# A woven forward pass: order of probability expansions, key blocks and row transposes, and the border to the next stage

## The chip, the core and the metric

The kernel runs on one core of one Trainium2 chip, in one launch. The core has five engines that work side by side: TensorE (PE in the profile, with its weight loads as PEld), VectorE (DVE), ScalarE (ACT), GpSimd (POOL) and SyncE (SP), which here only issues DMAs. PSUM, where TensorE writes its results, has eight banks, all in use in the stage that the change touches. The metric is the time on the device in microseconds (us), lower is better. A run gives one time; three runs of the kernel before are given below.

## The reference

The kernel computes the output of a gated mix of two attention branches, and the gradients of all its inputs but one for a given gradient of the output. There is one sequence of 2048 tokens of width 576.

```python
def _A_ref(x, wq, wk, wv, wo):          # 32 query heads of width 18, one shared key and value head
    q = (x @ wq).reshape(B, S, H, Dh).transpose(0, 2, 1, 3)
    k = x @ wk
    v = x @ wv
    p = softmax(einsum('bhqd,bkd->bhqk', q, k) * Dh ** (-0.5))
    o = einsum('bhqk,bkd->bhqd', p, v)
    return o.transpose(0, 2, 1, 3).reshape(B, S, H * Dh) @ wo

def _B_ref(x, mem0, Wq, Wk, Wv, Wo, seg_len):   # 32 heads of width 128, segments of 32 tokens
    mem = mem0                                   # 8 memory rows
    for s in range(n_seg):                       # 64 segments, each after the one before
        h = concatenate([mem, x[:, s * 32:(s + 1) * 32]], axis=1)
        q, k, v = (einsum('btd,dhe->bhte', h, W) for W in (Wq, Wk, Wv))
        p = softmax(where(mask, einsum('bhqe,bhke->bhqk', q, k) * scale, -1e9))
        o = einsum('bhqk,bhke->bhqe', p, v)
        o = einsum('bhte,hed->btd', o, Wo)
        mem = o[:, :8]                           # the memory of the next segment
        outs.append(o[:, 8:])
    return concatenate(outs, axis=1)

g = sigmoid((x * gate_w).sum(-1, keepdims=True))
out = g * _A_ref(...) + (1 - g) * _B_ref(...)
grads = vjp(out, grad_out)
```

Branch A is plain attention over all tokens. Branch B is a recurrence: the first eight output rows of a segment are the memory rows of the next one.

## The kernel before

The kernel goes through stages one after the other: preparation and the first projections; the *forward weave*; the *bulk* stage (`b_bulk`), which does branch B's token rows for all segments at once, forward and backward; a backward weave; and the weight gradients. The change touches the forward weave, its end and the start of the bulk stage.

**The weave.** `weave` (L282) runs two generators in turns. The *chain*, `b_chain_fwd` (L343), is branch B's recurrence over the memory rows: 64 segments in series, 16 portions each. The *sweep*, `a_pass1` (L1769), is branch A's forward attention, with row sums and the parts of dq that need the whole row: 64 blocks of 512 query columns, each over 16 tiles of 128 keys, so 1024 steps. Two sweep steps run first, then one portion of the chain and one sweep step alternate. With n the number of the sweep's step and j (0 to 15) the number of the portion in its segment, the portion just ahead of step n has j = n - 2 modulo 16. The order on each engine is the order in which the program issues (the stage is scheduled by hand): each engine works its instructions off in that order, and an instruction that waits holds up those behind it.

**A sweep step n** issues to PE: the two score matmuls of the *next* tile (`a_S`, one buffer of two banks), the two of the gradient (`a_dP`, three buffers), and, at its end, the accumulations of tile n-1 into `a_acc`. ACT takes the exponential of the next tile's scores (`a_E`, L1786, three buffers), DVE two products (`a_W`, L1819, two buffers). After each 16 tiles (n divisible by 16) ACT copies `a_acc` to `a_acs` (L1827), and a generator `a_post` (L1848) works on this block in four pieces, called from the sweep's steps: `half(0)` transposes two quarters of `a_acs` on PE into the PSUM tile `c_x` and copies them to `a_tk` on ACT; the second piece loads the block's queries with two transposing DMAs (L1859); `half(1)` transposes the other two quarters into `c_pj` and copies them on DVE (`evac` with `use="sv"[hf]`, L77 and L79 in the profile); the fourth piece does the arithmetic, on GpSimd but for one reciprocal. The transposes are at L1865. Before the change `half(0)` is called at the start of the steps with n = 3 modulo 16 and `half(1)` at the start of those with n = 14 modulo 16, ahead of everything else in the step; the other pieces are called at the end of steps 10 and 15 modulo 16.

**A segment of the chain**, by portions j, with the names of its tiles: 0, row sums of the segment before (`row_sums`, through `c_pj`, to the state `hm`, L320 and L323); 1 to 3, projection of the keys, `proj("k", 0, ...)` into `c_pj` and `proj("k", 1, ...)` into `c_x`, five blocks of four matmuls each; 4 to 6 the queries; 7 to 11 the values, with the scores in `c_x`, exponential `c_E`, denominators, `c_rd` (DVE) and probabilities `c_pn` (GpSimd) among them; in portion 10 the probabilities are spread to block-diagonal tiles by `expand` on GpSimd (L261): `PBm` for the memory keys, `PBx` for the token keys; 12, the output `po` in `c_x`, first eight matmuls with `PBx`, then eight with `PBm`; 13 to 15, `heads(0, 5)`, `heads(5, 11)`, `heads(11, 16)`: the output projection into `ph`, a tile in `c_pj`, four matmuls for each of its 16 indices. `c_pj` and `c_x` have one buffer (one bank) each, and the transposes of `a_post` are given the same two, since the pool that `a_pass1` gets as `xps` is the chain's.

**The border.** After the last sweep step the last block's `a_post` runs to its end at once, with its arithmetic on DVE (`eng`). In that case the query tile takes a buffer of `a_W`, and `a_tk` is the one buffer that the block before still uses. `b_bulk` (L669) then zeroes four tiles for block-diagonal memory rows (`x_vmB` and `x_kmB`, L675) on DVE, issues its first loads on SP (`load`, L709 for the token rows q, k, dO and v, in chunks of 16 heads, 512 KB each, L697 and L700 for the memory rows) and runs a loop over t, one group of four heads in each turn, software-pipelined over seven turns. In a turn, `trans` transposes the q, k, dO and v of a group on PE (`x_tr`, two buffers) and copies them to SBUF, dO and v on ACT, q and k on DVE; groups t for q and k, t - 2 for dO and v. `st_Om` at t - 3 is the first to read `x_vmB`, `st_Qm` at t - 5 the first to read `x_kmB`.

Of the kernel before, what the change touches and what calls it, by code (L numbers as in the profile page):

```python
# [12 lines left out]
BF16 = mybir.dt.bfloat16  # L13
F32 = mybir.dt.float32
U16 = mybir.dt.uint16
U32 = mybir.dt.uint32
P = 128

D = 576
# [27 lines left out]
class Kern:  # L47
# [295 lines left out]
    def b_chain_fwd(self, keep, sp, psum):  # L343
        nc = self.nc
        NSEG = self.NSEG
        hm = self.hm
        hx = keep.tile([P, 3, 64], F32, name="c_hx")
        PBm = keep.tile([P, 8, 64], BF16, name="c_PBm")
        nc.vector.memset(hx[:], 0.0)
# [63 lines left out]
        for s in range(NSEG):  # L413
# [26 lines left out]
            def proj(w, j, kts):  # L440
                if (w, j) not in pj:
                    pj[w, j] = psum.tile([P, 512], F32, name="c_pj" if w == "v" or j == 0 else "c_x", bufs=1)
                self.proj_part(pj[w, j], h_, self.W[w], j, kts)
                if kts[-1] == NKT - 1 and (w, j) != ("k", 1):
                    self.evac(flat(t2[w], j), pj[w, j][:], use="s")
# [17 lines left out]
            nc.gpsimd.tensor_copy(hist[:, :, s, :], h_[:, 0:NKT, 0:8])  # L463
            if not last:
                put_ride(s + 1)
            proj("k", 0, (0, 1))
            yield
            proj("k", 0, (2, 3, 4))
            proj("k", 1, (0,))
            if wt is not None:  # L470
                stash_end(*wt)
                wt = None
# [1 line left out]
                nc.gpsimd.dma_start(self.pq_dram[s // 4].rearrange("c i q s h x k -> (c i q) (s h x k)")  # L474
                                    .rearrange("p (n z) -> p n z", z=256), z4[:].unsqueeze(1).to_broadcast([P, 8, 256]))
            yield
            proj("k", 1, (1, 2, 3, 4))
            yield
            self.evac(flat(t2["k"], 1), pj["k", 1][:], use="s")
            proj("q", 0, (0, 1, 2, 3))  # L480
# [11 lines left out]
            src = self.mem_T(t2["q"], psum, "c_x", 1)  # L492
# [29 lines left out]
            pn = sp.tile([P, 2, 64], BF16, name="c_pn", bufs=1)  # L522
            nc.gpsimd.tensor_tensor(out=pn[:], in0=Et[:], in1=rd[:].unsqueeze(1).to_broadcast([P, 2, 64]), op=ALU.mult)
            PBx = sp.tile([P, 8, 4, 8], BF16, name="c_PBx", bufs=1)
            self.expand(PBm[:, :, 0:32].rearrange("p u (c q) -> p u c q", q=8), pn[:, 1].rearrange("p (u q) -> p u q", q=8), 8)
            self.expand(PBx[:], pn[:, 0].rearrange("p (u q) -> p u q", q=8), 8)
            nc.gpsimd.dma_start(self.pm_dram[s], pn[:].rearrange("p a b -> p (a b)"))
            proj("v", 1, (0, 1))
            yield
# [139 lines left out]
    def b_bulk(self, wp, vp, kp, sp, psum):  # L669
        nc = self.nc  # L670
        NTT = self.NTT
        mx = self.maskX
        mB = {w: [wp.tile([P, 4, 4, E], BF16, name=f"x_{w}mB{i}") for i in range(2)] for w in ("k", "v")}
        for t in mB["v"] + mB["k"]:
            nc.vector.memset(t[:], 0.0)  # L675
        mT = {}
        C = {}
        NG = NTT * 8
# [34 lines left out]
        BQ = 4  # L713
# [64 lines left out]
        def trans(t, w, nb):  # L778
            tt, g, r, d = view(t)
            pt = psum.tile([P, 4, P], BF16, name="x_tr", bufs=2)  # L780
            for i in range(4):
                self.tr(pt[:, i, :], d[w][:, 4 * (g % 4) + i, :], P)
            o = sp.tile([P, 4, P], BF16, name=f"x_{w}T", bufs=nb)
            self.evac(o[:], pt[:], use="s" if w in ("dO", "v") else "v")
            sc[w + "T", t] = o

        st_QT = lambda t: trans(t, "q", 2)
# [135 lines left out]
                 (5, st_K), (3, st_D), (5, st_KE), (3, st_O), (5, st_Q)]  # L923
        after = {st_O: (("vB", 0), ("v", 0)), st_D: (("mT", 0),), st_KE: (("q", 0), ("dO", 1)), st_Q: (("kB", 0), ("k", 3))}
        later = {}
        load(0, ("q", "k", "mT", "dO"))
        load(1, deep)
        load(0, ("v", "vB", "kB"))
        load(1, ("v", "vB", "kB"))
        load(2, deep + ("mT", "v"))  # L930
        for c in range(3, BQ):
            load(c, deep)
        for t in range(NG + 6):
            if t == NG - 8:
                self.sweep_first()
            sc["D"] = psum.tile([P, 512], F32, name="x_D", bufs=1)
            sc["Sb"] = psum.tile([P, 512], F32, name="x_S", bufs=1)
            for n, st in order:
                if n is None:
                    st(t)  # L940
                    continue
                if 0 <= t - n < NG:
                    st(t - n)
                if st in after and t - n >= 0 and (t - n) % 4 == 3:
                    c = (t - n) // 4
                    for w, wait in after[st]:
                        later.setdefault(t + wait, []).append((c + (BQ if w in deep else 3 if w in ("mT", "v") else 2), (w,)))
                        if wait == 0:
                            load(*later[t].pop())
            if t % 4 == 2 and t // 4 - 2 in range(NTT // 4):  # L950
                self.dl_rows(t // 4 - 2, sp, psum)
            for x in later.pop(t, ()):
                load(*x)
            flush(t >= NG)
# [814 lines left out]
    def a_pass1(self, keep, sp, psum, xps):  # L1769
        nc = self.nc  # L1770
        T, NTT = self.T, self.NTT
        NB = NPR * (T // 512)
        dl_all = self.dl_all
        S, E_, W_ = {}, {}, {}
        QD, load = self.QD, self.load_QD

        def mm_S(n):
            S[n] = psum.tile([P, 2, 512], F32, name="a_S", bufs=1)
            kt = n % 16
            for i in range(2):  # L1780
                r = slice(32 * i, 32 * i + 32)
                self.mm(S[n][:, i, :], lhsT=self.KV[r, kt * P:kt * P + P], rhs=QD[n // 16][r, :], tp=(32 * i, 0))

        def ex(n):
            E_[n] = sp.tile([P, 2, 512], BF16, name="a_E", bufs=3)
            nc.scalar.activation(E_[n][:], S.pop(n)[:], ACT.Exp, scale=SCALEA)  # L1786

        def acc_mm(acc, n, src, st, halves, first, last):
            t = src.pop(n)
            for h in halves:  # L1790
                for g in range(4):
                    self.mm(acc[32 * g:32 * g + 32, 256 * h:256 * h + 256],
                            lhsT=st[:, n % 16, 32 * h:32 * h + 32],
                            rhs=t[:, g % 2, 256 * (g // 2):256 * (g // 2) + 256],
                            start=first and h == 0, stop=last, tp=(0, 32 * g))

        mm_S(0)
        ex(0)
        NP_ = 16 * NB
        acc = None  # L1800
        post = None
        for n in range(NP_ + 1):
            if n < NP_:
                kt = n % 16
                if kt == 11:
                    load(n // 16 + 2)
                if post is not None and kt in (3, 14):
                    next(post)
                if n + 1 < NP_:
                    mm_S(n + 1)  # L1810
                dP = [psum.tile([P, 512], F32, name="a_dP", bufs=3) for _ in range(2)]
                for i in range(2):
                    r = slice(64 + 32 * i, 96 + 32 * i)
                    self.mm(dP[i][:], lhsT=self.KV[r, kt * P:kt * P + P], rhs=QD[n // 16][r, :], tp=(64 + 32 * i, 0))
                if n + 1 < NP_:
                    ex(n + 1)
                W_[n] = sp.tile([P, 2, 512], BF16, name="a_W", bufs=2)
                for i in range(2):
                    nc.vector.tensor_tensor(out=W_[n][:, i, :], in0=dP[i][:], in1=E_[n][:, i, :], op=ALU.mult)  # L1819
            if n > 0:  # L1820
                if n % 16 == 1:
                    acc = psum.tile([P, 512], F32, name="a_acc", bufs=1)
                acc_mm(acc, n - 1, E_, self.VK, (0, 1), n % 16 == 1, False)
                acc_mm(acc, n - 1, W_, self.WK, (1,), False, n % 16 == 0)
                if n % 16 == 0:
                    acs = sp.tile([P, 512], F32, name="a_acs", bufs=1)
                    nc.scalar.copy(acs[:], acc[:])  # L1827
                    bb = n // 16 - 1
                    QD.pop(bb)
                    post = self.a_post(bb, acs, sp, xps, dl_all)  # L1830
            if post is not None and n % 16 in (10, 15):
                if next(post, "end") == "end":
                    post = None
            yield
        for _ in post:
            pass
# [11 lines left out]
    def a_post(self, b, acs, sp, psum, dl_all):  # L1848
# [4 lines left out]
        eng = nc.vector if end else nc.gpsimd  # L1853

        def queries():
            qt = sp.tile([P, 2, 2, P], BF16, name="a_qt", tag="a_W" if end else "a_qt", bufs=2 if end else 1)
            src = self.qs_blk(b, 0)
            for a in range(2):
                nc.sync.dma_start_transpose(qt[:, a], src[a])  # L1859
            return qt  # L1860
# [5 lines left out]
            self.evac(tk[:, :, :, 32 * hf:32 * hf + 32], pt[:].rearrange("p t (g c) -> p t g c", c=32), use="sv"[hf])  # L1866

        if end:
            qt = queries()
        tk = sp.tile([P, 2, 4, 64], F32, name="a_tk", bufs=1)  # L1870
        half(0)
        yield
        if not end:
# [29 lines left out]
        r4 = sp.tile([P, 2, 2, 2, 2], F32, name="a_r4", bufs=2)  # L1903
        for w in range(2):
            eng.tensor_copy(r4[:, :, :, w, :], rl[:, w].rearrange("p t (a i) -> p a t i", i=2))
        q4 = qt[:].rearrange("p a t (b c) -> p (a t b) c", c=32)
        eng.tensor_tensor(out=q4, in0=q4, op=ALU.mult,
                                in1=r4[:].rearrange("p a t w i -> p (a t w i)").unsqueeze(2).to_broadcast([P, 16, 32]))
        dq_.dma_start(self.qs_blk(b, 1).rearrange("a p c -> p a c"), qt[:].rearrange("p a t x -> p a (t x)"))

    def sweep_first(self):
        self.QS = [self.wr.tile([P, 2, 512], BF16, name=f"b_QS{c}", bufs=1) for c in range(2)]
# [350 lines left out]
```

## Time and profile before

| | us |
|---|---|
| median of three runs | 5326.19 |
| the three runs | 5326.19, 5325.88, 5336.03 |
| the profiled execution | 5334.26 |
| its span, first to last instruction | 5332.5 |

Busy time by stage of the profiled execution (us; the stages' limits are read off the timeline):

| stage | from to | PE | DVE | ACT | POOL | DMA share |
|---|---|---|---|---|---|---|
| preparation, first projections | 0 to 420 | 386.69 | 171.27 | 149.49 | 72.32 | 0.60 |
| forward weave | 420 to 2060 | 1577.10 | 1419.32 | 1356.62 | 907.59 | 0.58 |
| border and bulk | 2060 to 2646 | 536.74 | 432.61 | 368.95 | 429.69 | 0.84 |
| backward weave | 2646 to 4307 | 1543.33 | 1405.07 | 1305.99 | 951.24 | 0.84 |
| the rest | 4307 to 5332 | 993.10 | 182.11 | 140.07 | 216.02 | 0.84, then 0.65 |

Busy time is when an engine has an instruction in work; matmuls overlap, so a busy PE need not be one at its peak. The table alone does not price an edit: for that one reads, for a single step, which instruction waits for which.

### The profile page before, as it was taken

To read this page: it belongs to the slowest core of one execution; us is meant where nothing else is said; L and a number is where in the kernel's file an instruction comes from. 1 tells how busy PE (TensorE), PEld (TensorE's weight loads), DVE (VectorE), ACT (ScalarE), POOL (GpSimd) and SP (SyncE) were. 2 spreads that over 40 slices of the span, in tenths; PEclk is the share of its full clock that TensorE was granted. 3 is DMA by queue.
4 is the path that set the end of the run, shared out by engine and by line. 5 is a ranking of instruction groups with operands and counts; after the bars stand their busy time and mean duration, and the time that the engine had idled before them with its cause. 6 is when DMAs were issued, how large, how long until landed. Compare 5 with 4: busy or idle time off the path is not lost. (4 is left out here: it accounts for less than half of the span.)

```text
span 5332.5 us, 214646 instructions
## 1 busy us (share of the span) xinstructions
PE 5036.9 (94%) x91428; PEld 2940.1 (55%) x91428; DVE 3610.4 (68%) x7146; ACT 3321.1 (62%) x4816; POOL 2576.9 (48%) x4890
## 2 busy tenths in 40 slices
PE   7999999999999998999889999999999999999999
PEld 6434555555555555777645555555544467764444
DVE  5337888888888887777678888888888831111112
ACT  4327888888888886666668888878877732111101
POOL 4004555555555555777746666666654321222223
PEclk9999999999999999999999999999999999999999
DMA  6645666656655445888867999899987778976653
GB/s 220 230 178 132 147 142 141 139 144 141 141 146 130 117 113 175 252 256 250 256 180 172 202 196 195 193 190 194 195 173 140 149 163 225 267 230 211 196 174 116
DMA packets 1115762, 961.21 MB, mean 180 GB/s; under 512 B 690738, under 2 KB 942139, under 8 KB 1105202
## 3 DMA queue, kind: packets, MB, share of 16 engines
q1 hardware_dynamic: 1013730, 702.18, 54.6%
q0 software_dynamic: 100928, 245.16, 15.7%
q8 instruction: 715, 11.71, 1.0%
q14 instruction: 245, 2.01, 0.1%
q10 hardware_dynamic: 144, 0.15, 0.0%
HBM read 521.16 MB, written 357.96 MB: 165 GB/s over the span
## 5 line engine op out<-in xcount | busy, mean ns | idle before, releaser
L1982 DVE TENSOR_TENSOR b_dS<-b_dP,b_E 128x512 bf16<-128x512 f32 x2048 | 1314.1, 683 | 235.6 <-issue 97.4
L1819 DVE TENSOR_TENSOR a_W<-a_dP,a_E 128x512 bf16<-128x512 f32 x2048 | 1313.3, 683 | 206.7 <-issue 74.6
L1959 ACT ACTIVATE b_E<-b_S 128x1024 bf16<-128x1024 f32 x1024 | 1047.8, 1023 | 298.5 <-PE b_dP L82 209.1
L1786 ACT ACTIVATE a_E<-a_S 128x1024 bf16<-128x1024 f32 x1024 | 1049.0, 1024 | 239.8 <-PE a_dP L82 192.6
L82 PEld LDWEIGHTS <-b_QS 32*128 32x128 bf16 (+1 forms) x8192 | 269.4, 92 | 529.8 <-issue 461.4
L82 PE MATMUL r_pj<-WT,r_dT 128*32 128x288 bf16 x12288 | 498.0, 287 | 8.4 <-issue 8.3
L82 PE MATMUL b_S<-b_KV,b_QS 32*128 32x512 bf16 x2048 | 406.6, 385 | 97.9 <-ACT b_E L1959 58.9
L82 PE MATMUL w_acc<-w_d,w_h 128*128 128x512 bf16 (+1 forms) x2400 | 473.8, 379 | 0.0
L82 PE MATMUL a_S<-a_QD,l_KV 32*128 32x512 bf16 x2048 | 399.5, 381 | 43.0 <-ACT a_E L1786 21.0
L82 PE MATMUL b_acc<-b_dS,b_QS 128*32 128x512 bf16 x2048 | 425.9, 394 | 0.2
L82 PE MATMUL a_acc<-a_E,l_VK 128*32 128x256 bf16 x8192 | 412.7, 278 | 5.2
L82 PE MATMUL b_acc<-b_E,b_QS 128*32 128x512 bf16 x2048 | 409.5, 395 | 1.5 <-issue 1.5
L82 PE MATMUL b_dP<-b_KV,b_QS 32*128 32x512 bf16 x2048 | 404.5, 390 | 0.0
L82 PE MATMUL a_dP<-a_QD,l_KV 32*128 32x512 bf16 x2048 | 398.4, 385 | 0.1
L82 PEld LDWEIGHTS <-r_dT 128*32 128x32 bf16 x12288 | 336.9, 97 | 100.7 <-issue 14.4
L82 PEld LDWEIGHTS <-w_h 128*128 128x128 bf16 (+1 forms) x2688 | 229.9, 100 | 258.4 <-issue 6.6
L82 PEld LDWEIGHTS <-l_KV 32*128 32x128 bf16 x4096 | 150.2, 91 | 288.5 <-issue 264.6
L82 PE MATMUL a_acc<-a_W,l_WK 128*32 128x256 bf16 x4096 | 291.4, 273 | 0.4 <-DVE a_W L1819 0.3
L79 ACT CAST w_o<-w_acc 128x512 bf16<-128x512 f32 x54 | 31.6, 585 | 384.3 <-PE w_acc L82 358.0
L77 DVE CAST w_o<-w_acc 128x512 bf16<-128x512 f32 x54 | 37.3, 691 | 335.2 <-PE w_acc L82 306.8
L82 PEld LDWEIGHTS <-l_VK 128*32 128x32 bf16 x8192 | 129.3, 94 | 237.1 <-issue 233.3
L1100 POOL TENSOR_TENSOR r_kb<-r_ks,bmask 128x512 bf16<-128x512 bf16 x176 | 188.7, 1072 | 146.6 <-DMA r_ks<-px_dram 59.1
(484 smaller groups left out, 10798.6 us busy)
## 6 DMA issues: line engine op xcount, KB each, us to landing
b_QS<-qs_dram SPq DMA_DIRECT2D x256, 256.0 KB
dOx_dram<-p_tok SPq DMA_DIRECT2D x16, 1024.0 KB
c_vx<-vx_dram SPq DMA_DIRECT2D x64, 256.0 KB
krow_dram<-c_k POOLq DMA_DIRECT2D x64, 256.0 KB
qrow_dram<-c_q POOLq DMA_DIRECT2D x64, 256.0 KB
vrow_dram<-c_v POOLq DMA_DIRECT2D x64, 256.0 KB
x_q<-qx_dram SPq DMA_DIRECT2D x32, 512.0 KB
x_k<-kx_dram SPq DMA_DIRECT2D x32, 512.0 KB
```

The lines of the kernel that those rows point to most:

```text
L77: nc.vector.tensor_copy(out, in_)
L79: nc.scalar.copy(out, in_)
L82: return self.nc.tensor.matmul(out, lhsT, rhs, start=start, stop=stop, tile_position=tp, skip_group_check=True)
L1100: nc.gpsimd.tensor_tensor(out=B[:], in0=a[:].unsqueeze(2).to_broadcast([P, 4, 4, SEG]), in1=self.bmask[:, :, 0].unsqueeze(1).unsqueeze(3). ...
L1786: nc.scalar.activation(E_[n][:], S.pop(n)[:], ACT.Exp, scale=SCALEA)
L1819: nc.vector.tensor_tensor(out=W_[n][:, i, :], in0=dP[i][:], in1=E_[n][:, i, :], op=ALU.mult)
L1959: nc.scalar.activation(E_[n][:], S.pop(n)[:], ACT.Exp, scale=SCALEA)
L1982: nc.vector.tensor_tensor(out=D_[n][:, i, :], in0=dP[i][:], in1=E_[n][:, i, :], op=ALU.mult)
```

## The change

Six edits, all in the order of work; what is computed stays the same.

1. In portion 10 `PBx` is spread ahead of `PBm`.
2. The key projections are split over portions 1 to 3 as three, four and three blocks, before as two, four and four.
3. `half(0)` is called at the end of the steps n = 2 modulo 16 (before at the start of the following one), `half(1)` at the end of the steps n = 14 modulo 16 (before at their start).
4. The last block's query tile is loaded five steps ahead of the sweep's end into a buffer of the chain's `c_wt`, whose weights are all through by then, and its `a_tk` takes a buffer of `a_E`.
5. In the bulk loop the four memsets and the loads that need them move into the turns t = 0 to 3 (`first`), one in each; the token rows v of chunk 0 are loaded ahead of chunk 1, and the loads of chunk 1's v and of the chunks 2 and 3 are issued from turns 0 to 2.
6. For t = 0 all copies of `trans` go to ACT.

```diff
--- before.py
+++ after.py
@@ -344,6 +344,7 @@
         nc = self.nc
         NSEG = self.NSEG
         hm = self.hm
+        self.cfs = sp
         hx = keep.tile([P, 3, 64], F32, name="c_hx")
         PBm = keep.tile([P, 8, 64], BF16, name="c_PBm")
         nc.vector.memset(hx[:], 0.0)
@@ -463,10 +464,10 @@
             nc.gpsimd.tensor_copy(hist[:, :, s, :], h_[:, 0:NKT, 0:8])
             if not last:
                 put_ride(s + 1)
-            proj("k", 0, (0, 1))
-            yield
-            proj("k", 0, (2, 3, 4))
-            proj("k", 1, (0,))
+            proj("k", 0, (0, 1, 2))
+            yield
+            proj("k", 0, (3, 4))
+            proj("k", 1, (0, 1))
             if wt is not None:
                 stash_end(*wt)
                 wt = None
@@ -474,7 +475,7 @@
                 nc.gpsimd.dma_start(self.pq_dram[s // 4].rearrange("c i q s h x k -> (c i q) (s h x k)")
                                     .rearrange("p (n z) -> p n z", z=256), z4[:].unsqueeze(1).to_broadcast([P, 8, 256]))
             yield
-            proj("k", 1, (1, 2, 3, 4))
+            proj("k", 1, (2, 3, 4))
             yield
             self.evac(flat(t2["k"], 1), pj["k", 1][:], use="s")
             proj("q", 0, (0, 1, 2, 3))
@@ -522,8 +523,8 @@
             pn = sp.tile([P, 2, 64], BF16, name="c_pn", bufs=1)
             nc.gpsimd.tensor_tensor(out=pn[:], in0=Et[:], in1=rd[:].unsqueeze(1).to_broadcast([P, 2, 64]), op=ALU.mult)
             PBx = sp.tile([P, 8, 4, 8], BF16, name="c_PBx", bufs=1)
+            self.expand(PBx[:], pn[:, 0].rearrange("p (u q) -> p u q", q=8), 8)
             self.expand(PBm[:, :, 0:32].rearrange("p u (c q) -> p u c q", q=8), pn[:, 1].rearrange("p (u q) -> p u q", q=8), 8)
-            self.expand(PBx[:], pn[:, 0].rearrange("p (u q) -> p u q", q=8), 8)
             nc.gpsimd.dma_start(self.pm_dram[s], pn[:].rearrange("p a b -> p (a b)"))
             proj("v", 1, (0, 1))
             yield
@@ -671,8 +672,6 @@
         NTT = self.NTT
         mx = self.maskX
         mB = {w: [wp.tile([P, 4, 4, E], BF16, name=f"x_{w}mB{i}") for i in range(2)] for w in ("k", "v")}
-        for t in mB["v"] + mB["k"]:
-            nc.vector.memset(t[:], 0.0)
         mT = {}
         C = {}
         NG = NTT * 8
@@ -781,7 +780,7 @@
             for i in range(4):
                 self.tr(pt[:, i, :], d[w][:, 4 * (g % 4) + i, :], P)
             o = sp.tile([P, 4, P], BF16, name=f"x_{w}T", bufs=nb)
-            self.evac(o[:], pt[:], use="s" if w in ("dO", "v") else "v")
+            self.evac(o[:], pt[:], use="s" if w in ("dO", "v") or t == 0 else "v")
             sc[w + "T", t] = o
 
         st_QT = lambda t: trans(t, "q", 2)
@@ -923,13 +922,22 @@
                  (5, st_K), (3, st_D), (5, st_KE), (3, st_O), (5, st_Q)]
         after = {st_O: (("vB", 0), ("v", 0)), st_D: (("mT", 0),), st_KE: (("q", 0), ("dO", 1)), st_Q: (("kB", 0), ("k", 3))}
         later = {}
-        load(0, ("q", "k", "mT", "dO"))
+        load(0, ("q", "k", "mT", "dO", "v"))
         load(1, deep)
-        load(0, ("v", "vB", "kB"))
-        load(1, ("v", "vB", "kB"))
-        load(2, deep + ("mT", "v"))
-        for c in range(3, BQ):
-            load(c, deep)
+
+        def first(t):
+            if t < 4:
+                nc.vector.memset(mB["vk"[t // 2]][t % 2][:], 0.0)
+                load(t % 2, ("vk"[t // 2] + "B",))
+            if t == 0:
+                load(1, ("v",))
+            elif t == 1:
+                load(2, deep)
+            elif t == 2:
+                load(2, ("mT", "v"))
+                for c in range(3, BQ):
+                    load(c, deep)
+
         for t in range(NG + 6):
             if t == NG - 8:
                 self.sweep_first()
@@ -947,6 +955,7 @@
                         later.setdefault(t + wait, []).append((c + (BQ if w in deep else 3 if w in ("mT", "v") else 2), (w,)))
                         if wait == 0:
                             load(*later[t].pop())
+            first(t)
             if t % 4 == 2 and t // 4 - 2 in range(NTT // 4):
                 self.dl_rows(t // 4 - 2, sp, psum)
             for x in later.pop(t, ()):
@@ -1804,8 +1813,11 @@
                 kt = n % 16
                 if kt == 11:
                     load(n // 16 + 2)
-                if post is not None and kt in (3, 14):
-                    next(post)
+                if n == NP_ - 5:
+                    self.qt_last = self.cfs.tile([P, D], BF16, name="c_wt", bufs=2)[:, 0:512].rearrange(
+                        "p (a t x) -> p a t x", a=2, t=2)
+                    for a, src in enumerate(self.qs_blk(NB - 1, 0)):
+                        nc.sync.dma_start_transpose(self.qt_last[:, a], src)
                 if n + 1 < NP_:
                     mm_S(n + 1)
                 dP = [psum.tile([P, 512], F32, name="a_dP", bufs=3) for _ in range(2)]
@@ -1828,7 +1840,9 @@
                     bb = n // 16 - 1
                     QD.pop(bb)
                     post = self.a_post(bb, acs, sp, xps, dl_all)
-            if post is not None and n % 16 in (10, 15):
+            if post is not None and n % 16 in (2, 14):
+                next(post)
+            elif post is not None and n % 16 in (10, 15):
                 if next(post, "end") == "end":
                     post = None
             yield
@@ -1853,7 +1867,7 @@
         eng = nc.vector if end else nc.gpsimd
 
         def queries():
-            qt = sp.tile([P, 2, 2, P], BF16, name="a_qt", tag="a_W" if end else "a_qt", bufs=2 if end else 1)
+            qt = sp.tile([P, 2, 2, P], BF16, name="a_qt", bufs=1)
             src = self.qs_blk(b, 0)
             for a in range(2):
                 nc.sync.dma_start_transpose(qt[:, a], src[a])
@@ -1866,8 +1880,8 @@
             self.evac(tk[:, :, :, 32 * hf:32 * hf + 32], pt[:].rearrange("p t (g c) -> p t g c", c=32), use="sv"[hf])
 
         if end:
-            qt = queries()
-        tk = sp.tile([P, 2, 4, 64], F32, name="a_tk", bufs=1)
+            qt = self.qt_last
+        tk = sp.tile([P, 2, 4, 64], F32, name="a_tk", tag="a_E" if end else "a_tk", bufs=3 if end else 1)
         half(0)
         yield
         if not end:
@@ -1903,10 +1917,11 @@
         r4 = sp.tile([P, 2, 2, 2, 2], F32, name="a_r4", bufs=2)
         for w in range(2):
             eng.tensor_copy(r4[:, :, :, w, :], rl[:, w].rearrange("p t (a i) -> p a t i", i=2))
-        q4 = qt[:].rearrange("p a t (b c) -> p (a t b) c", c=32)
+        qt = qt if end else qt[:]
+        q4 = qt.rearrange("p a t (b c) -> p (a t b) c", c=32)
         eng.tensor_tensor(out=q4, in0=q4, op=ALU.mult,
                                 in1=r4[:].rearrange("p a t w i -> p (a t w i)").unsqueeze(2).to_broadcast([P, 16, 32]))
-        dq_.dma_start(self.qs_blk(b, 1).rearrange("a p c -> p a c"), qt[:].rearrange("p a t x -> p a (t x)"))
+        dq_.dma_start(self.qs_blk(b, 1).rearrange("a p c -> p a c"), qt.rearrange("p a t x -> p a (t x)"))
 
     def sweep_first(self):
         self.QS = [self.wr.tile([P, 2, 512], BF16, name=f"b_QS{c}", bufs=1) for c in range(2)]
```

## What is expected: the prediction

> **What bounds the kernel now.** I read the page's busy table first (TensorE has work for 94% of the span), then the stretches by stage, then the timeline of single steps, since a mean over the span cannot price an edit inside one step. Two stretches of the table by windows, with span, PE, PEld, DVE, ACT and POOL busy, granted clock, DMA share and GB/s, and the border between the forward weave and the bulk stage beneath:
>
> ```profile
> 440.00:800.00 360.00, 346.97 (x7750) 189.66 (x7750) 312.80 (x564) 299.30 (x396) 199.32 (x459) 1.00 0.63 141
> 1600.00:2040.00 440.00, 424.44 (x9440) 231.65 (x9443) 381.53 (x690) 364.96 (x482) 239.28 (x552) 1.00 0.47 116
> 2060.00:2080.00 20.00, 5.59 (x76) 4.43 (x77) 11.05 (x28) 2.21 (x5) 11.29 (x17) 0.50 0.93 297
> ```
>
> In the weave no engine is full: PE 96%, DVE 87%, ACT 83%. At the border PE does 5.6 us of work in 20 us, at half the granted clock, while DMA runs at 0.93.
>
> The weave's steps are all visible as starts of the two a_S matmuls (one pair per step). Over the segment from 1199.75 they lie 1.55, 1.55, 1.55, 1.55, 1.58, 1.55, 1.84, 1.56, 1.55, 1.55, 1.55, 1.60, 1.63, 1.63, 1.63, 1.63 us apart: 25.50 us, and the 63 intervals between the first and the last a_acs copy (448.2 and 2058.2) give 25.56. A segment near 702 and one near 1503 show the same list, but for one step of 1.83 in the latter. The value 1.55 is a floor: a_S starts, 0.48 us later the exponential starts, runs 1.02 us, and the next a_S may enter the one a_S buffer about 0.05 us after that. Only steps whose TensorE work is longer stand above it. A step has about 0.67 us of the sweep's own PE work (from a_S to the chain's first matmul: 1219.39 less 1218.73), 0.22 us for each block of four projection matmuls (1219.39, 1219.82, 1220.04) and about 0.1 us back to a_S; four blocks make 1.63.
>
> The timeline (start, duration, engine, line, operation, count, idle before) from the step where the token values are read. I number steps by the sweep's index modulo 16; a step's interval runs from its a_S to the next, so step 13's begins at 1209.08, step 14's at 1210.92:
>
> ```profile
> 1208.88 0.63 POOL L261 TENSOR_TENSOR c_PBm<-c_pn,bmask 128x256 bf16<-128x256 bf16 x1
> ...
> 1209.08 0.39 PE L82 MATMUL a_S<-a_QD,l_KV 32*128 32x512 bf16 x2
> ...
> 1209.46 0.63 POOL L261 TENSOR_TENSOR c_PBx<-c_pn,bmask 128x256 bf16<-128x256 bf16 x1
> ...
> 1210.15 0.35 PE L82 MATMUL c_x<-c_PBx,c_vx 128*128 128x32 bf16 x8 [0.23 <-POOL c_PBx L261]
> ...
> 1210.35 0.39 PE L82 MATMUL c_x<-c_PBm,c_v 128*128 128x64 bf16 x8
> ...
> 1210.58 0.41 PE L1865 MATMUL c_pj<-identF,a_acs 128*128 128x128 f32 x2
> ...
> 1210.92 0.39 PE L82 MATMUL a_S<-a_QD,l_KV 32*128 32x512 bf16 x2
> ...
> 1211.10 0.42 DVE L77 COPY a_tk<-c_pj 128x256 f32<-128x256 f32 x1 [0.21 <-PE c_pj L1865]
> ...
> 1211.44 1.29 DVE L1819 TENSOR_TENSOR a_W<-a_dP,a_E 128x512 bf16<-128x512 f32 x2
> ...
> 1211.59 0.79 PE L82 MATMUL c_pj<-WoN,c_oT 128*32 128x288 bf16 x20
> ...
> 1212.48 0.39 PE L82 MATMUL a_S<-a_QD,l_KV 32*128 32x512 bf16 x2
> ```
>
> Read four things in it. PE waits 0.23 us for c_PBx, the second of two expansions. The sweep's second pair of row transposes writes c_pj ahead of a_S. Its copy runs on DVE ahead of step 14's two products a_W. And heads, 20 matmuls at 1211.59, write c_pj as well, long after that copy is done.
>
> **Part by part, for a segment.** *Expansions swapped.* PBx would be ready at 1209.51 instead of 1210.09, PBm at 1210.09 instead of 1209.51. The first eight matmuls then start where the sweep's work ends (about 1209.75), the other eight at 1210.15, and end near 1210.38. With the transposes gone from this step, a_S could come at 1210.48, so the floor decides: 1.55 for 1.84, **-0.29 us**. If the second wait reaches a_S, -0.15.
>
> *Second pair of transposes to the end of step 14.* They now stand behind the sweep's accumulations, and right ahead of heads. Heads' tile has c_pj's only buffer, so its first matmul waits for the a_tk copy. That copy is issued behind both products of step 14 on DVE, which runs in the order of issue. Times from the a_S of step 14 at 1209.08 + 1.55 = 1210.63: the products start 0.52 later (1211.44 less 1210.92), at 1211.15, and take 1.29, to 1212.44; the copy follows 0.08 before their end as now, 1212.36 to 1212.78; PE is released 0.06 later (the last a_W ends at 2057.79 and its matmul starts at 2057.85). Heads start at 1212.84. The transposes end near 1211.30 + 0.37 = 1211.67, so PE stands for about 1.15 us, with heads, the next a_S and all after it queued behind. Heads take 20 x 0.03 = 0.6 us (its 20 weight loads take 0.57), 0.1 to a_S: 1213.55. The step is 2.92 for 1.56, **+1.36 us**. Nothing hides it: ACT and DVE then wait for a_S and a_dP, and no later step can be under 1.55. Bounds: +1.05 if the copy starts 0.3 earlier than reckoned, +1.5 if the gaps of the step of 1.83 come on top.
>
> *First pair and keys.* The pair moves from behind the two k blocks to ahead of them, in the same interval (step 2), so the move itself costs nothing there; a_tk's ACT copy stays between the same two exponentials. But this step takes three key blocks for two: 1.60 + 0.22 = 1.82. Step 3 keeps four blocks. Step 4 has three for four: 1.63 to the floor, 1.55. Together **+0.14 us**; bounds +0.02 (a gap of 0.1 before the transposes closes) and +0.21.
>
> Sum: -0.29 + 1.36 + 0.14 = +1.21 us. Heads follow the transposes in segments 1 to 62: 62 x 1.21 = **+75 us**. Bounds 62 x (1.05 - 0.29 + 0.02) = +48 and 62 x (1.5 - 0.15 + 0.21) = +97.
>
> *Border.* What ends each wait of PE there now:
>
> ```profile
> 2061.98 0.42 DVE L77 COPY a_tk<-c_pj 128x256 f32<-128x256 f32 x1 [4.07 <-POOL a_t L1899]
> ...
> 2070.25 0.91 DVE L675 MEMSET x_kmB<- 128x1024 uint32 x1 [0.16 <-issue]
> ...
> 2071.49 0.59 PE L87 MATMUL x_tr<-identB,x_q 128*128 128x128 bf16 x4 [5.13 <-DVE x_qT L77]
> ...
> 2078.47 0.61 PE L87 MATMUL x_tr<-identB,x_v 128*128 128x128 bf16 x4 [3.88 <-DMA x_v<-vx_dram]
> ```
>
> The last block's a_tk in a buffer of the a_E ring starts 2.4 us earlier (its transposes end about 2059.5). The first tile's q and k copies go to ACT, idle then, and one memset instead of four (1.07 us from start to start) stands ahead of the next ones: DVE is free for those at about 2065.6 for 2072.1. But then x_v ends the wait: it is issued at 2064.86, behind three 512 KB loads of the next chunk; ahead of them, at about 300 GB/s, it lands 3 x 1.7 = 5.2 us earlier. The query transposes, on SP until 2059.45, are issued five steps earlier, so all loads may leave SP up to some 6 us sooner if nothing but the queue holds them, which no row shows. Against that, three memsets go into steps 1 to 3 of the bulk loop, and SP's loads of chunks 2 and 3 wait behind the masked-row loads that wait for them. I take **-7 us**, between the 5.2 and the sum of both, and bounds of -12 and +3 (3 x 1.07, if they all show and the loads gain nothing).
>
> The profiled execution took 5334.26 us, its span is 5332.5; the median of the three runs is 5326.19, 8 us below it. Span: 5332.5 + 75 - 7 = 5400.5. On the median: 5326 + 68 = **5394 us**.
>
> **Rivals.** *No wait at heads.* Then step 14 is 0.67 + 0.37 + 0.1 + 0.6 + 0.1 = 1.84, +0.28, a segment -0.29 + 0.28 + 0.14 = +0.13, in all 62 x 0.13 - 7 = +1: **5327 us**, no change; if step 2 gives its 0.14 back too, about 5318. It decides where step 14 costs less than 0.26 us more than now, so the copy would have to be done by about 1211.7, ahead of both products. For it: today's copy starts as soon as its transposes are done. Against: today it is issued ahead of the products, and DVE's rows follow the issue order throughout. 5 in 100.
>
> *The clock drops in each wait.* At the border, after a gap of 4.8 us, four x_tr transposes take 0.61 us at a clock of 0.50 where they take 0.40 at 1.00. If the 2.9 us of PE work in steps 14 and 15 ran at half clock, that is up to 2 us a segment more: 5394 + 124 = **5518 us**. Against: after a gap of 1.58 us at 2100.42 the four transposes still take 0.40. The Trainium skill (TensorE: Matmul & The Clock Gate, The HAM clock gate) puts the drop after an idle window of about 3.4 us, which agrees with both gaps here; its section on psum-queue depth-cycling, though, lets frequent short waits on PSUM buffers make the clock oscillate, which is what this rival would be. 4 in 100.
>
> *The border gives nothing,* since DMA is full there (0.93 share) and x_v still ends the wait: 5326 + 75 = **5401 us**. 6 in 100.
>
> **How the numbers follow.** The forecast has 85 in 100. With the border's bounds its range is 5326 + 48 - 12 = 5362 to 5326 + 97 + 3 = 5426; I take 5360 to 5426, which holds the third rival and leaves out the first two. About 0.2%, 10.7 us, is what a measurement of this kernel can tell from no change: slower 0.95, and of the first rival's share 0.03 within it and 0.02 faster.
>
> **What would show it.** In the changed trace: heads' c_pj matmuls idle about 1.1 us on DVE a_tk, 62 times; a_tk<-c_pj starting behind two a_W; the c_PBx wait of PE (14.2 us in all) gone; a_acs copies 26.8 us apart; the clock 1.00 throughout the weave; no wait of PE for x_v near 3.9 us. If the a_acs copies lie 25.6 us apart, the wait isn't there and the forecast is wrong; if the weave's clock falls below 1.00, the second rival holds.

## The result, and the profile after

| | before | changed |
|---|---|---|
| median | 5330.31 us | 5406.02 us |
| lowest to highest | 5325.88 to 5336.03 | 5403.06 to 5412.49 |
| span of the profiled execution | 5332.5 us | 5404.4 us |

The changed kernel is slower by 1.4%: ratio 1.0141, 95% interval 1.0129 to 1.0154, some 76 us. (The kernel before was run again beside the changed one, which moved its median from 5326.19 to 5330.31.)

Where the 71.9 us between the two spans lie, by marks that both timelines have:

| from | to | before | changed | difference |
|---|---|---|---|---|
| first a_acs copy | last a_acs copy (63 blocks) | 1610.0 | 1690.8 | +80.8 |
| last a_acs copy | first exponential of the bulk stage | 14.7 | 4.3 | -10.4 |
| first exponential | last exponential of the bulk stage | 554.4 | 571.6 | +17.2 |
| last exponential | last accumulation of the backward weave | 1679.2 | 1664.9 | -14.3 |

The first line is the weave, and the second the border. The four differences add up to 73.3; the rest of the program took 1.4 us less. The last two are not the change's work alone: both stages vary from kernel to kernel by such amounts (*The border alone*, below).

The stretches of the changed kernel that answer to those shown of before (span, PE, PEld, DVE, ACT, POOL busy, granted clock, DMA share, GB/s); the border now lies 80 us later:

```profile
440.00:800.00 360.00, 336.33 (x7360) 183.01 (x7362) 297.69 (x539) 282.13 (x375) 191.21 (x441) 1.00 0.58 134
1600.00:2040.00 440.00, 411.87 (x9002) 223.40 (x9005) 362.65 (x656) 343.89 (x457) 235.81 (x544) 1.00 0.49 117
2140.00:2160.00 20.00, 10.71 (x165) 9.10 (x165) 14.21 (x43) 5.59 (x12) 14.71 (x23) 0.59 0.82 262
```

All three engines of the weave lost ground, PE from 347 to 336 us in the first stretch, DVE from 313 to 298, ACT from 299 to 282: no engine became full, and all three stand idle for longer. The clock stays at 1.00. At the border PE does 10.7 us of work in 20 for 5.6.

Steps 13 and 14 of a segment in the changed kernel's timeline, the answer to the rows shown of before. Step 13 begins with the first a_S, step 14 with the second:

```profile
1219.96 0.63 POOL L261 TENSOR_TENSOR c_PBx<-c_pn,bmask 128x256 bf16<-128x256 bf16 x1
...
1220.41 0.39 PE L82 MATMUL a_S<-a_QD,l_KV 32*128 32x512 bf16 x2
...
1220.55 0.63 POOL L261 TENSOR_TENSOR c_PBm<-c_pn,bmask 128x256 bf16<-128x256 bf16 x1
...
1221.18 0.37 PE L82 MATMUL c_x<-c_PBx,c_vx 128*128 128x32 bf16 x8
...
1221.96 0.39 PE L82 MATMUL a_S<-a_QD,l_KV 32*128 32x512 bf16 x2 [0.17 <-ACT a_E L1795]
...
1222.48 1.29 DVE L1831 TENSOR_TENSOR a_W<-a_dP,a_E 128x512 bf16<-128x512 f32 x2 [0.26 <-ACT c_oT L543]
...
1222.73 0.44 PE L1879 MATMUL c_pj<-identF,a_acs 128*128 128x128 f32 x2
...
1223.69 0.41 DVE L77 COPY a_tk<-c_pj 128x256 f32<-128x256 f32 x1
...
1224.16 0.80 PE L82 MATMUL c_pj<-WoN,c_oT 128*32 128x288 bf16 x20 [0.99 <-DVE a_tk L77]
...
1224.89 0.39 PE L82 MATMUL a_S<-a_QD,l_KV 32*128 32x512 bf16 x2
```

The transposes start at 1222.73 and would be ready for their copy half a microsecond later (0.55 us, in the run *The copy ahead of the products* below). The copy starts at 1223.69, 0.08 us ahead of the recorded end of the two products (1222.48 + 1.29). Heads start 0.06 us after its end, having held PE up for 0.99 us, and the next a_S stands behind heads. Step 13 is 1.55 us now, step 14 2.93.

From the waits between 440 and 2110 us (who waits for whom, us in total, times, longest):

```profile
PE c_pj L82 <- DVE a_tk L77: 60.1, 61, 1.0
...
PE c_x L82 <- POOL c_PBm L261: 0.7, 3, 0.2
```

The first is new, 61 waits of about 1 us; with the one behind this window they are 62, 61.1 us in all. The second is what is left of the 14.2 us that PE waited for an expansion.

### The profile page after: what moved, and what is told of

The parts are those of the page before. It is cut to its first block, busy times and chain, and to the rows that moved or that the text cites. A ratio compares the mean times of both kernels' runs of the same rounds, so it can differ in the third digit from the quotient of the medians.

```text
span 5404.4 us, 214473 instructions
## 1 busy us (share of the span) xinstructions
PE 5051.7 (93%) x91250; PEld 2951.4 (55%) x91428; DVE 3608.8 (67%) x7144; ACT 3312.7 (61%) x4818; POOL 2577.4 (48%) x4890
```

## The experiments

All are compared with the kernel before, run on the same chip. "A block" is the distance of the first and the last a_acs copy over 63, in the profiled execution.

**The second pair back.** In the changed kernel, only `half(1)` returns to the start of its step.

```diff
+                if post is not None and kt == 14:
+                    next(post)
                 if n + 1 < NP_:
                     mm_S(n + 1)
...
-            if post is not None and n % 16 in (2, 14):
+            if post is not None and n % 16 == 2:
```

> The changed kernel with its second pair of transposes back at the start of step 14, everything else as changed. Theory (heads wait for the pair's copy, which stands behind two products on DVE): steps 13 and 14 are 1.57 to 1.65 and 1.55 us, the wait of heads for a_tk is gone, a block of the weave takes 25.5 to 25.6 us (26.84 changed, 25.56 before), and the whole is within 10 us of before (5315 to 5332). Rival (the cost lies in the longer step 2 and in the swapped expansions): the kernel stays slower than before by more than 50 us.

Measured: 5333.25 us for 5334.65, ratio 0.9996 (0.9986 to 1.0006). A block takes 25.58 us, step 13 1.64, step 14 1.55, and of PE's waits on c_pj for a copy none is left. The same place (the step's a_S starts at 1209.88):

```profile
1210.06 0.42 DVE L77 COPY a_tk<-c_pj 128x256 f32<-128x256 f32 x1
...
1210.55 0.79 PE L82 MATMUL c_pj<-WoN,c_oT 128*32 128x288 bf16 x20
```

The copy is over at 1210.48, and heads start without a wait. The whole loss is gone with this one edit, and so is the rival. (The time lies 1 us above the 5315 to 5332 that was expected, on a chip on which the kernel before took 5334.65.)

**The second pair alone**, in the kernel before:

```diff
-                if post is not None and kt in (3, 14):
+                if post is not None and kt == 3:
                     next(post)
...
-            if post is not None and n % 16 in (10, 15):
+            if post is not None and n % 16 == 14:
+                next(post)
+            elif post is not None and n % 16 in (10, 15):
```

> The kernel before with nothing but the second pair moved to the end of step 14. Theory: step 13 falls from 1.84 to about 1.60, step 14 goes from 1.56 to 2.9; a block takes 26.6 to 26.75 us, the whole 66 to 74 us more than before (5396 to 5404). Rival (the pair alone is harmless, the cost comes with the other edits): under 20 us more.

Measured: 5401.97 for 5334.65, ratio 1.0138 (1.0125 to 1.0152), 67 us. A block takes 26.66 us, step 13 1.59 (median), step 14 2.92; the wait of heads is there 62 times, 61.3 us. Together with the run before, the loss is placed from both sides: without this edit it is gone, and this edit alone gives 67 of the 76 us.

**The copy ahead of the products.** The changed kernel; on PE the order stays, on DVE the two products of step 14 are issued after the copy.

```diff
-                W_[n] = sp.tile([P, 2, 512], BF16, name="a_W", bufs=2)
-                for i in range(2):
-                    nc.vector.tensor_tensor(out=W_[n][:, i, :], in0=dP[i][:], in1=E_[n][:, i, :], op=ALU.mult)
+                def products():
+                    ...
+                late = post is not None and kt == 14
+                if not late:
+                    products()
...
             if post is not None and n % 16 in (2, 14):
                 next(post)
+                if n % 16 == 14:
+                    products()
```

> The changed kernel, but in step 14 the two products are issued on DVE behind the pair's copy; the order on PE is as changed. Theory (it is the place in DVE's queue): the copy starts 0.5 us after the transposes, step 14 falls from 2.92 to about 2.5 us, with heads' wait at 0.5 to 0.6 for 0.99; 62 x 0.42 = 26 us less than the changed kernel (about 5380). Rival (what costs is handing c_pj over at this place on PE, whatever DVE's order): step 14 stays at 2.9 and the time at 5406.

Measured: 5386.85 for 5334.65, ratio 1.0103 (1.0086 to 1.0119). That is 52 us above the kernel before, for 76: 24 less, where 26 had been expected. Step 14 takes 2.52 us, a block 26.49 for 26.84. The same place in its timeline (the step's a_S starts at 1211.74):

```profile
1212.51 0.44 PE L1886 MATMUL c_pj<-identF,a_acs 128*128 128x128 f32 x2
1213.06 0.42 DVE L77 COPY a_tk<-c_pj 128x256 f32<-128x256 f32 x1 [1.06 <-PE c_pj L1886]
...
1213.40 1.28 DVE L1832 TENSOR_TENSOR a_W<-a_dP,a_E 128x512 bf16<-128x512 f32 x2
1213.54 0.80 PE L82 MATMUL c_pj<-WoN,c_oT 128*32 128x288 bf16 x20 [0.58 <-ACT c_vmT L79]
```

The copy now starts 0.55 us after the transposes, not 0.96, and heads again 0.06 us after its end (1213.48). The profile names an ACT copy of c_x as what released heads; that copy ends 0.03 us later and works on another bank, so it is a case of several ends close together, not a second cause: in the next run heads start 0.22 us before that copy ends. In each of the 62 segments heads start 0.051 to 0.054 us after the end of the a_tk copy, here, there and in the changed kernel. 0.41 of the 1.36 us are thus the place in DVE's queue. What is left, transposes and copy between the accumulations and heads, stays whatever the order on DVE. Heads in a bank of their own were not tried: all eight are in use.

**The copy on ACT.** The changed kernel with `use="ss"[hf]` for `use="sv"[hf]`.

> The changed kernel with the second pair's copy on ACT in place of DVE, at the same place in the order. Theory (the copy waits for whatever is queued ahead on its engine: on ACT the exponential of step 14, which ends 1.50 us after a_S): the copy runs from 1.50 to 1.87, heads start at 1.93, step 14 takes 2.66 us for 2.92; 16 us less than the changed kernel, about 5390. Rival (the wait belongs to the handing over of c_pj): 2.92, no change.

Measured: 5391.94 for 5333.63, ratio 1.0099 (1.0072 to 1.0126). Step 14 takes 2.54 us, 0.12 less than expected: its a_S is at 1210.26, and the copy starts 0.10 us ahead of the exponential's recorded end (1211.75), as the copies on DVE start 0.08 ahead of that of the products:

```profile
1210.73 1.02 ACT L1795 ACTIVATE a_E<-a_S 128x1024 bf16<-128x1024 f32 x1 [0.16 <-PE a_dP L82]
...
1211.65 0.37 ACT L79 COPY a_tk<-c_pj 128x256 f32<-128x256 f32 x1
...
1211.90 0.39 ACT L79 CAST c_vmT<-c_x 128x256 bf16<-128x256 f32 x1
...
1212.07 0.80 PE L82 MATMUL c_pj<-WoN,c_oT 128*32 128x288 bf16 x20 [0.61 <-ACT a_tk L79]
```

So the copy runs from 1.39 to 1.76 after a_S where I had reckoned 1.50 to 1.87. (The cast shown is the copy of c_x of the run before; heads start while it runs.) Heads wait for whichever engine has the copy, by as much as that engine has queued ahead of it.

**The swapped expansions alone**, in the kernel before.

> The kernel before with the swapped expansions alone. Theory: step 13 falls from 1.84 to 1.64 us, no wait of PE for an expansion, 62 x 0.2 = 12 us less (ratio 0.9977). Rival: the other eight matmuls wait as long for the second expansion, step 13 stays above 1.75, no change.

Measured: 5318.63 for 5327.28, ratio 0.9983 (0.9972 to 0.9994). Step 13 takes 1.64 us, a block 25.36 for 25.56: 63 x 0.19 = 12 us by the timeline, 9 by the times.

**The first pair alone**, in the kernel before (`half(0)` to the end of step 2, keys in 2, 4, 4).

> The kernel before with the first pair of transposes alone moved, from behind the key blocks to ahead of them. Theory (a change of tile form on PE in either direction costs about 0.1 us, and this order has one more of them before a_S): step 2 goes from 1.60 to 1.68 us, 5 us more in all. Rival, the prediction's own reading (the move costs nothing): step 2 stays at 1.60.

Measured: 5336.68 for 5327.28, ratio 1.0014 (1.0005 to 1.0023). Step 2 takes 1.68 us, a block 25.65: 6 us in all by the timeline, 9 by the times. PE in step 2, first in the kernel before, then in the changed kernel, which has three key blocks there (x12):

```profile
1217.13 0.39 PE L82 MATMUL a_S<-a_QD,l_KV 32*128 32x512 bf16 x2
...
1217.81 0.61 PE L82 MATMUL c_pj<-Wk,hm 128*32 128x512 bf16 x8
1218.36 0.44 PE L1865 MATMUL c_x<-identF,a_acs 128*128 128x128 f32 x2
1218.73 0.39 PE L82 MATMUL a_S<-a_QD,l_KV 32*128 32x512 bf16 x2
```

```profile
1202.48 0.39 PE L82 MATMUL a_S<-a_QD,l_KV 32*128 32x512 bf16 x2
...
1203.24 0.44 PE L1879 MATMUL c_x<-identF,a_acs 128*128 128x128 f32 x2
1203.61 0.83 PE L82 MATMUL c_pj<-Wk,hm 128*32 128x512 bf16 x12
1204.38 0.39 PE L82 MATMUL a_S<-a_QD,l_KV 32*128 32x512 bf16 x2
```

Read the form behind each MATMUL: 128*32 is a matmul on a strip of 32 columns, 128*128 one on the whole array, 32*128 one on a strip of 32 rows. From the accumulations (128*32 too) to the keys there is no gap, from two key blocks (0.43 us, as from 1219.39 to 1219.82 in the kernel before) to the transposes 0.12, from the transposes (0.37) to a_S none. In the changed order the transposes come 0.76 after a_S where the keys came after 0.68, and from three key blocks (0.65) to a_S there is 0.12 again. So each end of work in strips of 32 columns costs about 0.1 us, and the moved pair makes two such ends out of one; that the other direction costs as much, as the expectation had it, these rows don't show. The Trainium skill (TensorEngine Tiling (Array Packing), Key Properties) says that a change of the tiling mode drains TensorE; the rows agree with that where the strips end and show no gap where the transposes end. Why the two differ was not tried.

**The keys alone**, in the kernel before.

> The kernel before with the keys in 3, 4, 3 alone. Theory: step 2 goes from 1.60 to 1.82, step 4 from 1.63 to 1.55, 0.14 us a block or 9 us in all. Rival (the block just changes its step): no change in the sum of the steps 2 to 4, 4.86 us.

Measured: 5335.75 for 5327.28, ratio 1.0014 (1.0003 to 1.0024). Steps 2 to 4 take 1.82, 1.63, 1.55, a block 25.70: +0.14 us, 9 us in all by the timeline and 8 by the times.

**The border alone**, in the kernel before (edits 4 to 6).

> The kernel before with the three edits of the border alone. Theory: the first exponential of the bulk stage comes 9 to 11 us earlier after the last block's row sums, the fifth about 5 us; the whole gains 5 us (5 to 10). Rival (the bulk stage gives it back, as in the changed kernel's profile, where the lead is gone by the middle of that stage): no change within 3 us, with the bulk stage 5 to 14 us longer than before.

Measured: 5333.50 for 5334.65, ratio 0.9998 (0.9986 to 1.0009). Exponentials of the bulk stage, us after the last a_acs copy:

| | 1st | 3rd | 5th | 9th | 33rd | last |
|---|---|---|---|---|---|---|
| before | 14.7 | 24.5 | 32.2 | 50.7 | 155.9 | 569.1 |
| expansions alone (border as before) | 14.7 | 24.9 | 32.7 | 50.3 | 155.1 | 568.9 |
| second pair alone (border as before) | 14.7 | 23.6 | 31.4 | 49.0 | 155.2 | 578.5 |
| border alone | 3.4 | 16.9 | 27.4 | 44.1 | 151.4 | 579.5 |
| changed kernel | 4.3 | 17.0 | 27.1 | 44.9 | 152.2 | 576.0 |

The lead is 11 us at the first exponential, 5 at the fifth and about 4 at the 33rd. The stage then takes 576.1 us for 554.4 from its first exponential to its last. At the end of the stage kernels with the same border differ by 10 us, and on the mean nothing is left of it: the last exponential comes at 573.8 in the five kernels of all these runs with the border of before, at 573.9 in six with the changed one (without the last run below, whose profiled execution was its slowest). From the last a_acs copy to the end of the program the former take 3262.9 to 3274.4 us, mean 3269.4, the latter 3262.4 to 3276.4, mean 3270.5. That is what the rival says, but the scatter of 10 us could hide a gain of 4 or 5, and the interval of the time (7.5 us less to 4.8 more) holds both.

**The changed border with the swapped expansions**, without the pairs and the keys.

> The kernel before with the swapped expansions and the border's edits, without the moved pairs and the keys in 3, 4, 3. Theory (the two edits add up, step 13 at 1.64 as with the second pair put back): a block takes 25.35 us, the weave 12 us less, the border's net gain 0 to 5: 12 to 17 us less than before (ratio 0.9968 to 0.9978). Rival (the freed 0.2 us is eaten by the wait for the second expansion or elsewhere in the weave): within 5 us of before.

Measured: 5312.77 for 5327.28, ratio 0.9974 (0.9964 to 0.9984). This version beats both kernels, by 14.5 us the one before. From the run with the expansions alone, on the same chip, it differs by the border's edits only: 5312.77 for 5318.63, 6 us less. That is their largest gain on record, but the executions of the latter lie between 5307 and 5331, so it is not certain.

**The first probabilities on DVE**, on top of that, to find what eats the lead. In the changed kernel's border, whose x_v no longer holds PE up:

```profile
2148.90 0.63 PE L87 MATMUL x_tr<-identB,x_v 128*128 128x128 bf16 x4
...
2151.93 0.79 POOL L1924 DMA_DIRECT2D qs_dram<-c_wt  x1
2152.67 0.69 POOL L824 TENSOR_TENSOR x_P<-x_E,x_r 128x256 bf16<-128x256 bf16 x1
2153.41 0.10 PEld L87 LDWEIGHTS <-x_P 128*128 128x128 bf16 x1 [3.27 <-POOL x_P L824]
2153.42 0.29 PE L87 MATMUL x_S<-identB,x_P 128*128 128x128 bf16 x1 [3.01 <-POOL x_P L824]
```

GpSimd still issues the weave's last DMAs, the line shown being the last of a row of them that starts at 2146.44, and x_P stands behind them.

```diff
-            nc.gpsimd.tensor_tensor(out=o[:, t % 4], in0=Et[:], in1=bc(rl[:]), op=ALU.mult)
+            (nc.gpsimd if t else nc.vector).tensor_tensor(out=o[:, t % 4], in0=Et[:], in1=bc(rl[:]), op=ALU.mult)
```

> The swapped expansions and the border's edits, and the probabilities of the bulk stage's first group on DVE in place of GpSimd. Theory (there GpSimd still issues the weave's last DMAs, and x_P behind them holds PE up for 3 us): PE's wait of 3 us for x_P is gone, the fifth exponential of the bulk stage comes 2 to 3 us earlier after the last row sums than without it; 2 to 3 us less, which the time may not tell (ratio 0.997). Rival (another wait takes its place, a load of the masked rows): the fifth exponential comes as before.

Measured: 5321.21 for 5333.63, ratio 0.9975 (0.9961 to 0.9988), no better than without it. The wait for x_P is gone and the third exponential comes at 14.3 us, not 16.9. But the fifth comes at 29.2, not 27.4 (in an execution of 5340 us, the slowest of this kernel):

```profile
2062.66 0.67 POOL L824 TENSOR_TENSOR x_P<-x_E,x_r 128x256 bf16<-128x256 bf16 x1
2069.93 0.61 POOL L886 TENSOR_TENSOR x_Y<-x_P,x_dl 128x256 f32<-128x256 bf16 x1 [6.60 <-DMA memT_dram<-memT_hist]
2070.63 0.72 POOL L888 TENSOR_TENSOR x_dS<-x_X,x_Y 128x256 bf16<-128x256 f32 x1
2071.31 0.67 POOL L749 TENSOR_TENSOR x_PTB<-x_PT,tmask 128x256 bf16<-128x256 bf16 x1
...
2072.03 0.64 PE L82 MATMUL x_po<-x_v,x_PTB 64*64 64x128 bf16 x8 [4.07 <-POOL x_PTB L749]
```

Now x_Y is reached early, and waits 6.6 us for a DMA that the weave's end issued (the profile puts it down to the 640 KB of memT_hist); x_PTB is queued behind it, and PE waits 4.07 us for that. The rival held, with another wait than the one it named. But the later fifth exponential isn't the edit's doing alone: with the second pair back, where x_P still stands on GpSimd, x_Y waits 5.0 us for the same DMA and the fifth comes at 30.1. In all seven kernels with the changed border x_Y starts 19.7 to 21.9 us after the last a_acs copy, whether x_P starts at 10.4 (here) or at 13.6 to 13.7 (the six others). What x_Y shares with memT_hist was not tried.

## Why the prediction was right

**Second pair.** Right, in mechanism and size: step 14 at 2.92 us, as forecast; heads idle 0.99 us for 1.15, 62 times. The wait is shorter because the transposes start 0.77 us after a_S, not 0.67, and their record is longer (0.44 for 0.37); its end, set by DVE, is where it was reckoned (2.20 after a_S for 2.21), and that alone sets the step. Two runs place the loss on this edit, two others 0.4 us of it on the queue ahead of the copy.

**Expansions.** Right in the sum: step 13 came down to the floor of 1.55. But the -0.29 us is not the swap's alone. The pair's leaving by itself brings 1.84 to 1.59, the swap by itself to 1.64; the two gains overlap at the floor, and beside the moved pair the swap is worth 0.04.

**First pair and keys.** Step 4 went to 1.55 as said. The step that failed is "so the move itself costs nothing there": step 2 took 1.90, not 1.82. The gaps around work in 32-column strips had been taken as one constant 0.1 us a step; they depend on what stands next to what, and the move alone costs 0.08. Together +0.22 us a block, not +0.14, and just beyond the bound of +0.21.

**The sum of the weave.** 1.28 us a block instead of 1.21, so 80.8 us instead of 75: the 0.08 of the first pair over 62 blocks is 5 us of it.

**Border.** The term of -7 us is not borne out. Its parts came as worked out, and more: the first exponential came 10.4 us earlier, with no wait of PE for x_v. But it left out who works on the other side: GpSimd's queue, full of the weave's DMAs, held PE up for 3.0 us in their place. About 4 us are left by the 33rd exponential, and on the mean of the traces nothing at the end of the stage; by the times the edits gain 1 us alone and 6 beside the swapped expansions. How much they gain in all stays open.

**The rivals.** No wait at heads: fell, 61.1 us are there. The clock: fell, 1.00 in both stretches of the weave, with a wait of 1 us in every 26.8; the rule on short waits on PSUM buffers (the Trainium skill, TensorE: Matmul & The Clock Gate, A second HAM failure mode: psum-queue depth-cycling) does not show here. A border that gives nothing: not excluded, and the means of the traces speak for it.

**The total.** 5406 us was measured, 12 above the forecast and 76 above a median of before that itself rose by 4. So 8 of the 12 are the change's (76 for 68), and the weave's 6 us are most of them. The span came out closer, at 5404.4 for 5400.5, by luck: from the last a_acs copy to the end the changed kernel took 8.9 us less than the one before in this pair of executions, about the border's term, where other pairs of kernels with these two borders lie as far apart in either direction.

## What to carry to other kernels

When a piece of work that borrows a single buffer is moved, look at who takes that buffer next on the same engine, and at what stands ahead of the copy that frees it on the engine that makes the copy: here 0.37 us of transposes, put right ahead of the bank's next user, cost 1.36 us, where at the start of the step their copy had passed ahead of the products and nobody had waited for it. In a loop with a floor, add up each step and compare with the floor: moving work out of a step that then rests at the floor saves only down to it, while the step that receives it pays in full.

## What the runs showed of the hardware that was not expected

Ending work in strips of 32 columns of TensorE costs about 0.1 us before the next form (0.12 from keys to transposes and from keys to a_S, 0.08 from accumulations to transposes), while transposes on the whole array are followed without a gap. The bulk stage, with the same instructions, took 554 to 565 us between its first and its last exponential in five kernels whose border is that of before. A DMA that GpSimd issued took 0.57 to 1.69 us of its queue in the changed kernel's border, and the row of them from 2146.44 on held x_P, and PE with it.
